# Joint norms of unit pairs in three attention phases, with a new order table, in an attention and gated two-layer kernel

## The chip, the cores and the metric

The kernel runs on one core of one Trainium2 chip. The metric is the device time of one execution in microseconds (us); less is better. Before the change the median of three runs is 299.85 us (299.45 to 300.24).

## The reference

Inputs `q`, `k`, `v` have shape 8 x 8 x 576 x 64 (batch, heads, sequence, head size). Attention is causal with a window of 128 positions and a linear position bias per head; its output, 4608 tokens of 512 values, goes through two matrix products with `h * cos(h)` between them.

```python
scores = scale * q @ k.T                              # per batch and head
mask   = (rel >= 0) & (rel < 128)                     # rel = query pos - key pos
attn   = softmax(where(mask, scores + slope[h] * -abs(rel), -1e9))
x      = (attn @ v) -> 4608 x 512
h      = x @ w_in                                     # 512 -> 2048
out    = (h * cos(h)) @ w_out                         # 2048 -> 512
```

## The kernel before, in words

**Work units.** The attention of one batch is cut into nine units. A unit `(b, pr, G)` is a pair of heads `pr` (0 to 3) and a half `G` of the first 512 queries; the ninth, `(b, "t", None)`, holds the last 64 queries of all heads. A unit goes through `scores` (TensorE, lines 529 and 539), `exps` (ScalarE, 590 and 598), `mask` (VectorE multiplies by the band and the bias, 611 and 623), `pv` (TensorE, 640 to 656, with a column of ones in `v` that gives the sum of each row), and the norm: a reciprocal of the row sums and a multiplication, both VectorE reading PSUM. `norm` does it for one unit (694 and 696, or 681 and 684 for the tail unit), `norm_two` for two units at once (710 and 712). The result `xnat` is turned into `xT`, either by TensorE and a copy (`x_pe`, 729 and 742, copies at 752 on ScalarE or 753 on VectorE) or by a transposing DMA on SP's queue (`x_dma`, 768), which is used where the tokens are not needed in the very next stage.

**Pairs and banks.** `attention` takes the units two at a time. Their `pv` write PSUM banks 2 and 3 (the list `UB`); two `pv` of a pair are one operation unless one unit is a tail. A pair is normed jointly in the phases listed in `JN`, and only where it holds no tail unit. A joint norm keeps both banks until its multiplication is done, and takes two neighbouring `xnat` buffers.

**Stages.** The 4608 tokens are nine chunks of 512. For each chunk c: the first product with `w_in` and the cosine (`moe1`, 782, 787, 791; `moe1_half`, 975, for chunk 0; `moe1_fast`, 876 to 943, with fewer products for the last chunks), then phase c of attention with a quota of units (8, 10, 10, 12, 14, 9 for phases 0 to 5, after 9 units of a start phase), then the second product with `w_out` (`moe2`, 1161, or `moe2_fast`, 1067 and 1138, with the operand sums at 1031 and 1046). Attention of phase c and the second product of chunk c are interleaved on TensorE.

**The start.** The first rows of `q` come by SP's queue (363) and are cast by VectorE (367) and ScalarE (368); the others and `k` come by POOL's queue (356). TensorE transposes them against the identity made by POOL (420, 421), and ScalarE (500) or VectorE (501) copies them out as `qt` and `kt`. Then come the first scores, exponentials (with the masks made at 460 and 465), `pv`, norms and transposes, and the first matmuls with `w_in` (975).

**The order.** All operations are recorded first, in program order, with their data, buffer and bank dependencies. Then `follow` reads `TABLE`: a packed list of the numbers of all operations in the order in which they are issued, with one bit more for each copy that may run on ScalarE or on VectorE (set: VectorE). Each engine runs its operations strictly in that order, waiting on semaphores. The table thus sets the order on TensorE, VectorE, ScalarE, and of the transfers on POOL's and SP's queues, for the whole kernel.

Of the kernel before, what the change touches and what calls it, by code (L numbers as in the profile page):

```python
# [8 lines left out]
ALU = mybir.AluOpType  # L9
# [7 lines left out]
NBLK = 5  # L17
# [10 lines left out]


TABLE = (  # L30
    'c-nPV2Y6If7JmPfH!Wo*A%PHdEHqifjs=k}tV#(GFqBXPBn4$bu`FK_%_4*%1ObV(K#D*JSt&-E!h-'
    '0xDvPKfD@{Z`QYO7kX6D^JciMYzU|;fHUhcd1+;jf_Kj&N_3_w#jJy552L+3%Pc;zlP#H-yktj(-'
    'pEjqM{ck}PJwCrB3q-'
    '{9M;&d$5qHR9WADS}~;_2H1xbO#`q+wdtgon`B>6%HyG|f?3%VnDsdnr<5N0St5ZZ)?8zmXNGD<Zg2=y6N`U+Gy?'
    '$F$*GyJWJoN!r+3anTS_iMU&FrmJy)q1{k##U*rYHRJHq^Dy35b!Y@oPU}o$A?_9;n<O%5Xs0l2&{m^^1BgNm_9P'
    '~pqObs4C1TN&{Qy{6(86~%nA#%H5NW^O=4`d2vLnc~h(_}2&mQcz_^`@$G{b79x#rnLjt-93Hcj0-'
    'yv%|m2e+*e0cZK}!+72b)WUaJT8@pXD+fk0N6bOV1gB(Si4?NA5T2-'
    '!JB(zEKr!Mj%{>;HUNYjab!Z7$qCql;L3G!CjefR+FFk(bw73vr<2ntCbb8MB)_5dQYyf6J%<J=0tY;ul(MgN&rc'
    'O0s&EiG$uIcm#Y~Vab;v#yqnaVrE7GY>V-A}Btqa`;P_Nv&jvF#{*7WM`>VMkre&#)Wy?uO_aV#gax-'
    'm{4=v5trFP6j>R?Tw2c0rY#J*M(j<PaOY>o)>#w^hUa2)xJ2kX>J~-'  # L40
    '#3SczLYEI#)13`0UMgZCvSU&r@KXVhQx8AYHOt^~S#t385v1pL)39f1&X4(!RY_VSn%~;N7Le~0Vt5k)3C!7qncH'
    'Sb_KKyP6<WQBL=(H{om`}^2hwehkBNkN1f6-'
    '=6Jf`#n1*9F&|{#~8ip5b`?XFO3>mnmKg4fqM&X#D2BXTu`vb#MxEL-'
    '2=FZh<=U!>)?uhVjo~ev?pC0h90j^d!W2#$W>Vg}3Lez;yMB~`dF58D5!*GHZ4bkokcrZJo8XMBIs3+J`c0!*&!='
    'cNak2M(+9t6%k<c;_TI5&xT-;_~SjMe)zLQ?kr-'
    '9G)}so_oZgT~!nS)>B%(>F{i(nL<%Kma6dPT_kIY8xqVGm@6sSZY)QY;}3kyZHF!JjrNbPWohF6A1kpQae^Jz>4Y'
    'nMq|4ag_#Z%abX$X0Qx{bdg5-'
    'w!C^Sy0wzSSv6YO*7!5g5KOZPW>L)jeqDWi^PVfHiNt_&bV&I7<#pb?el1f*R3lvbBscPqQM6(|M=#E!7MQtWiEo'
    '^$q8jetWg{{laSk`ID;w6<lHL!It@CI3ZRWxET-dy=6bdfZi^BN)-'
    'kx6rkxYh^Af7Y$CX%W0qP@nf!;+_cuy#JAV$$(>L5)aS8M@n1a32RRL3Yb{W0a`!VJ8|o4{JEnxs(L});p(&v8a9'  # L50
    'u_yO{KZHL$YuW?tu(Sy-'
    '!vCGTmAdZpg4wXLtycpkG<<E5@OtDZg=!_1h1+Njmjw*z0aL)7QnhFOPv(elHPlI>oe%EXgvk}suL+RHI+l!oPEe'
    'ttc)y)KY7q-'
    'GO9HpEp~!82*s>_!_J5TR{@5f%EL7h^Wh(4l4fbO%j~jd783&`#My06C4>3;+Is6L%3tT|^hYe#$tr1&iB&6{dwW'
    'wmj!;Baz_4=p8Jja_9ps>tY{=<;GUvOwSAXGq+K`;>!KNrH|ImXY(ASTzHFN^apdvpSj*r6^VK)$8H@P=`NPcPO&'
    'XkYSBhFw`irt0gqb!LQPqlVQC7VwU?z)4yP6n<)+6xUk=rH29r)HJ=#nkkufV0J5o_@v9wsQWd0@&P$WT0e*0vOC'
    'WIl=#9la*x}LDtWaQG=0xl2(#f%Kz3QWi+K|tR$xwKh#_K~ywPUk>V_~X988-'
    'dL$7M*|kTUzrMQ~>ttJm@GYT>9QFLiQ#JGHIu^Q5UX9joXGsV+1N~s5tf4rg&Z0t843@yK)VUZ;eO{vvf>bj#_<{'
    'E{YJE13lG{)N}UY3D6Y>lsCkRX4ja{$9_e$IQETy;j`zD56VwIGwJ{vRRhIkkY72;<?OL;WxyDsbjLJ`d?#gik4L'
    '%OwvOj>3X-Yk5pe`ia}jeHouYwjx-lYe?zUO*6w~{=z!E<7?VOdoJcyIBk3;YN22T&Udsl*?z2EoT*eN`VQ(2lOw'  # L60
    '$ie!%Cd#CND}y^H-5G~apWoVM#%(x$>q1=4UeA7@v$>FHVpXpRNz-`z1w9-2S&rNI|0<^yIkuIxJ1&2qr-'
    'yn-P&*BAkwbEg<YgZWM`B<Ux7!?;yxT0hEB9Poq9_H<xB+6$<+&1*V*jXQ=!i##UhbBC-HxJ9b4f>O5FQM$GVlYY'
    '0;EzOMeT$+Oi@ir?~G>em;QF`Fb7Uw0-'
    ')DSUv5QX5E;wvHsQX@ok50m+CO*%wR0XM0gH$JNq(o?|pd}rcrfU%@Ny^NS$EwY}9WNlRrb}CwAb0!CyUIkX8zeE'
    't`lBMNi5`Z9289jS-byN0#8`Z0-K46!6u51NJvfI*I<pVOKD}#Bep<(EjKAJ>#OvyA?}aT-'
    'Eb<QtZWG>gAiq@nZu|-Z>5YIIxXgTPJ-Qv8(%8OF{x~utj?J<T~4~q=Mu!G!`B%o{U^X7EYfMjy|cFw5l`KlR}P!'
    'Ka8_mW<8uzKs|eA|5Ic*_e7cdlcU3q+K^v!GU5I4-4igxj^A<ASLge=;<iQSZL!w7=WR?W#-'
    'vXhCLeN@7x(>g+{qRDABl6lLS<Fw>!h`LQKaFe(HMu)ipAva=P&;AW;|7_8}?>Xa&1&CWqRI3oTyJm0VHkMj~b-'
    'KU~R;VLVn(IO$x|2XD-#Cwa~YvoxGM@0FUnOnlZXB(9|3jhMQu{ARUV7(DVnyPJ@o)_f&pP-'
    '0v1&I@q5tK0fHEZqW2B6vpePz;Nsr3p!)OwvLraMQ%IB0%b!Fk8kvD!^ICX(d5SU`>)JBl;A)3x!^A~*gA1H!Njk'  # L70
    '9bb31AJ#9jLnSFn5nJP8V+>6WI*{{9$K=-'
    'Ii4(}ekB>9rlTbz8;dAV@$vsGY#Mm*p3)v9cI)0mEeyn;9Sk1Ej+_{IEB=6m(OWM%qp|L4FkV=POcUwRSz4?%tjO'
    '!EE7%nJVFo1y$1xLEKDW3+%V*`a_(LEi!<eA{Ja22J?)4@RI|7PRIIN8a6UkTIrQNx^0MmIX}Gdse33v8*ibI3(}'
    'Q6!`hQq7VFL0TWDyL%1z)LEb|Fqa2QJsRyz<9M$)jGC(Gyq6mu#GUiIyWiMn}lrw_vC^2CnX65Kq(JOA5auqsW#('
    'az6gPr;3Fs3vS*iFTO!lleCE-fW~K`s@;f-'
    'DuL7*vWwMFvwo)YDYK%Ys!&lL=}a$qa_Dqe_$j$%4|P%7Sk&C^p7|E-05OoaEoQU{w(_HKhuIl)N)0L6E?If-ndQ'
    'f>bOkomPRMj6=zXYB;2Fs8S$=8>KAS9bxj%$jo92RQykW$_h$ynL-'
    ';1n|B~0C{NjJ5M;#~HD{_qDyS92ASr8Q=(}$hf?wlN8Dh7U35CEE3Rb4eZHcVrLB=YO&ys+EVM&F9-'
    '>_E|awkyN8>TE$>Y^ZLfm%hXRv?#4)t*Y5EYzr4%5w1xWK3uw7gWYn<tfyI;9|8HRZ>;#t145fwkp%W<gb}oO8Vt'
    ';%~TDI391Zd3iT@kVuEmcuME+!AOkCeh?Xh408{MGRAGcvK=>2_;SOCz;Xi5FXBMh@##BcNK~)Hu608vNLvl*BDH'  # L80
    'GHNRFy;B3gs%n{7pj$fl+x7VWHhmHY6$LK<1t&5`BViq8BRfR0)!TR`@J<FZkbrVSDq@w=+*W79u-'
    'AsdYv9Vyey(st|R(RU84Bg0wsI(4aO|@>6G)${!)5eW-e@5K<&=Z_fWO<s>k5KMFa_g&GrXJ7L|{Z-'
    'kIjkN?mA0G*W>_y'
)


# [9 lines left out]
class Plan:  # L96
# [18 lines left out]
    def op(self, eng, fn, r=(), w=(), dma=None, occ=100, lat=None, pri=5, mode=0, table=None, two=False):  # L115
        o = Op()
        o.two = two
        o.seq = len(self.all)
        o.eng = (eng,) if isinstance(eng, str) else tuple(eng)
        f = fn[0] if isinstance(fn, list) else fn["act"] if isinstance(fn, dict) else fn  # L120
        o.grp = "/".join((self.now, f.__code__.co_qualname.split(".")[-3],
                          o.eng[0] if dma is None else "dma"))
        o.soft = pri < 5
        pri = self.PRI.get(o.grp, pri)
        o.fn, o.r, o.w, o.dma = fn, tuple(r), tuple(w), dma
        o.occ, o.lat, o.pri, o.mode, o.table = occ, occ if lat is None else lat, pri, mode, table
# [24 lines left out]
        self.all.append(o)
        return o
# [7 lines left out]
    def follow(self, text):  # L160
# [5 lines left out]
        for lo, hi in zip(raw[:n], raw[n:]):  # L166
            at = (at + lo + 256 * hi) % 65536
            o = self.all[at % 32768]
            if isinstance(o.fn, dict):
                e = "dve" if at >= 32768 else "act"  # L170
                o.fn, o.eng = o.fn[e], (e,)
            self.order.append(o)

# [79 lines left out]
def bass_alibi_sliding__then__act_gcu_kernel(  # L253
# [8 lines left out]
    with ExitStack() as ctx:  # L262
# [596 lines left out]
        def moe1_fast(c, f4):  # L859
# [358 lines left out]
        identity()
        load_qk("q", q, 0, 1)
        load_qk("k", k, 0, 1)  # L1220
        constants()
        load_v(0, range(2))
        load_w_in(0)
        load_v(0, range(2, NBLK - LORD))
        masks()
        for n in range(2):
            qk_transposes(0, "q", n, 0, OB)
            qk_transposes(0, "k", n, 0, UB)
        for u in range(1, 4):
            load_w_in(u)  # L1230
            if u == 1:
                load_v(0, range(NBLK - LORD, NBLK))
# [92 lines left out]
```

## Time and profile before

| what | value |
|---|---|
| median of three runs | 299.85 us |
| profiled execution: its own time | 299.71 us |
| profiled execution: span of its instructions | 298.0 us |
| VectorE busy | 262.1 us (88%), 522 instructions |
| ScalarE busy | 222.1 us (75%), 318 instructions |
| POOL busy | 95.2 us (32%), 122 instructions |
| TensorE clock granted | full in every stretch |
| first matmul starts, last matmul starts | 5.70 us; about 295 us |

The span runs from the first to the last instruction. The profiled execution's own time is 1.7 us longer than its span. PE is TensorE's matrix multiplication, PEld its weight load, which overlaps the matmul before; DVE is VectorE, ACT is ScalarE, POOL is GpSimd, SP the engine that only issues transfers. A row of the timeline gives the start, the length, the engine, the line, the tiles and the count of merged instructions, and in brackets how long the engine had been idle and what released it.

### The profile page before, as it was taken

The page shows a single profiled execution, that of the slowest core. Times are in us where ns is not written, and L with a number is a line of the kernel's source. Part 1 is how long each engine was busy: PE and PEld are TensorE (multiplying, and loading weights), DVE is VectorE, ACT ScalarE, POOL GpSimd, SP SyncE. Part 2 cuts the span into 40 slices and gives each one's busy share as a digit, 9 for nine tenths or more (in the row PEclk, how much of TensorE's full clock was granted, in tenths as well). Part 3 has the DMA queues.
Part 4 walks back from the last instruction along what each step waited for, and adds up shares of the span by engine and source line. Part 5 has one row for each costly group of instructions (what it writes and reads, how often), then busy time and mean ns, then how long its engine had stood idle before and what let it go on. Part 6 is the DMA issues. An engine that isn't in the chain of part 4 may idle for free.

```text
span 298.0 us, 7278 instructions
## 1 busy us (share of the span) xinstructions
PE 287.9 (97%) x2974; PEld 205.2 (69%) x2974; DVE 262.1 (88%) x522; ACT 222.1 (75%) x318; POOL 95.2 (32%) x122
## 2 busy tenths in 40 slices
PE   2899999999999999999999999999999999999996
PEld 2678845446874586458854788547768888888884
DVE  3879877599977999899999999999999999999972
ACT  5788878689757889688777878579778758778620
POOL 7997000599642303991195005000000000000000
PEclk9999999999999999999999999999999999999999
DMA  7999999999999994999999939973131400041033
GB/s 153 173 205 208 207 169 146 180 196 155 136 175 147 130 187 90 142 173 173 169 170 133 163 85 130 159 164 74 21 79 21 150 2 0 2 141 37 10 134 106
DMA packets 147729, 37.96 MB, mean 127 GB/s; under 512 B 133360, under 2 KB 146416, under 8 KB 147696
## 3 DMA queue, kind: packets, MB, share of 16 engines
q0 software_dynamic: 99344, 18.10, 79.7%
q1 hardware_dynamic: 48352, 19.41, 34.5%
q8 instruction: 23, 0.38, 0.5%
q14 instruction: 10, 0.08, 0.1%
HBM read 36.70 MB, written 9.44 MB: 155 GB/s over the span
## 4 chain that ended last, share of the span: by engine, by line
PE 94%; DVE 2%; POOL 1%; issue 1%; ACT 1%; POOLq 0%; DVEq 0%
PE ps L1067 33%; PE ps L782 24%; PE ps L876 11%; PE ps L539 5%; PE ps L975 5%; PE ps L1161 4%; PE ps L653 3%; PE ps L656 2%; PE ps L742 2%; PE ps L483 2%; PE ps L529 1%; DVE kt L501 1%; PE ps L640 1%; PE ps L642 1%; PE ps L1138 1%
## 5 line engine op out<-in xcount | busy, mean ns | idle before, releaser
L1067 PE MATMUL ps<-w_outb,gT 128*128 128x256 f16 x512 | 82.3, 273 | 0.0
L782 PE MATMUL ps<-xT,w_inb 128*128 128x512 f16 x336 | 82.2, 379 | 0.0
L787 ACT ACTIVATE cos<-ps,halfpi 128x512 f32<-128x512 f32 x84 | 54.9, 687 | 18.9 <-PE ps L782 13.9
L598 ACT ACTIVATE p<-ps 128x768 bf16<-128x768 f32 (+1 forms) x64 | 55.6, 915 | 11.5 <-PE ps L539 9.5
L791 DVE TENSOR_TENSOR gT<-ps,cos 128x512 f16<-128x512 f32 x84 | 54.5, 686 | 5.5 <-ACT cos L787 5.1
L1067 PEld LDWEIGHTS ps<-w_outb,gT 128*128 128x128 f16 x512 | 48.2, 98 | 12.5 <-issue 1.3
L782 PEld LDWEIGHTS ps<-xT,w_inb 128*128 128x128 f16 x336 | 31.7, 98 | 31.1 <-DVE gT L791 1.5
L375 POOL DMA_DIRECT2D vp<-in_v_dram x40 | 34.3, 892 | 53.1 <-PE ps L656 35.3
L1067 PE MATMUL ps<-wsum,gsum 128*128 128x256 f16 x256 | 38.5, 273 | 0.0
L623 DVE TENSOR_TENSOR p<-p,emask 128x768 bf16<-128x768 bf16 (+1 forms) x64 | 38.0, 615 | 0.3
L385 POOL DMA_DIRECT2D qnat<-in_q_dram x30 | 25.5, 918 | 23.9 <-DMA qt<-qnat 23.9
L1052 ACT ACTIVATE ob<-ps 128x512 f32<-128x512 f32 x33 | 19.6, 598 | 13.7 <-PE ps L1067 11.2
L385 POOL DMA_DIRECT2D knat<-in_k_dram x30 | 25.7, 948 | 9.3 <-DMA kt<-knat 7.0
L1067 PEld LDWEIGHTS ps<-wsum,gsum 128*128 128x128 f16 x256 | 23.2, 98 | 4.0 <-issue 0.5
L876 PE MATMUL ps<-xT,w_inb 128*128 128x256 f16 x132 | 24.8, 273 | 0.0
L696 DVE TENSOR_TENSOR xnats<-ps,rec 128x256 f16<-128x256 f32 x56 | 21.9, 420 | 0.5
L539 PE MATMUL ps<-qt,kt 64*128 64x128 bf16 (+1 forms) x320 | 20.1, 253 | 1.3 <-DVE kt L501 1.3
L653 PEld LDWEIGHTS ps<-vp,p 128*128 128x128 bf16 x256 | 16.0, 99 | 4.3 <-issue 1.0
L653 PE MATMUL ps<-vp,p 128*128 128x65 bf16 x256 | 18.9, 196 | 0.1
L1067 PE MATMUL ps<-wsum,gT 128*128 128x256 f16 x112 | 18.1, 273 | 0.0
L539 PEld LDWEIGHTS ps<-qt,kt 64*128 64x128 bf16 x320 | 11.9, 98 | 8.6 <-issue 3.6
L1161 PE MATMUL ps<-w_outb,gT 128*128 128x512 f16 x64 | 17.6, 380 | 0.0
(111 smaller groups left out, 478.0 us busy)
## 6 DMA issues: line engine op xcount, KB each, us to landing
out_dram<-ob SPq DMA_DIRECT2D x35, 256.0 KB, 2.7
vp<-in_v_dram POOLq DMA_DIRECT2D x32, 128.0 KB, 6.9
qnat<-in_q_dram POOLq DMA_DIRECT2D x24, 128.0 KB, 7.1
knat<-in_k_dram POOLq DMA_DIRECT2D x24, 128.0 KB, 10.8
w_inb<-in_moe_w_in_dram POOLq DMA_DIRECT2D x4, 512.0 KB, 10.5
w_outb<-in_moe_w_out_dram POOLq DMA_DIRECT2D x4, 512.0 KB, 21.8
gsum<-in_q_dram POOLq DMA_DIRECT2D x1, 576.0 KB, 15.5
gsum<-in_k_dram POOLq DMA_DIRECT2D x1, 576.0 KB, 17.6
```

The costliest lines, as they stand in the source:

```text
L375: op("pool", [lambda e, t=t, rows=rows: e.dma_start(vp[b % 2][0:rows, t, :, 0:64], v[b, :, 128 * t:128 * t + rows, :].rearrange("h p d -> ...
L385: fns.append(lambda e, t=t, rows=rows: e.dma_start(nat[which][b % 2][0:rows, t, :, :], src[b, :, 128 * t:128 * t + rows, :].rearrange("h p ...
L539: ins = e.matmul(ps[:, banks[x], c0:c1], keys_ap(b, x, pr, kc), query_ap(b, x, pr, qb, 128 * nb), start=c0 == 0 and (b, pr, G) not in seed ...
L598: op("act", lambda e: e.activation(P[i][:, :, 0:hi], src_[:, :, 0:hi], ACTF.Exp, scale=0.125), w=held + [("P", i)], occ=920 if G else 691, ...
L623: op("dve", lambda e: e.tensor_tensor(p, p, m, ALU.mult), r=[("EM", h0), ("EM", h1)] + ([] if G else [("EM2", h1)]), w=[("P", i)], occ=600 ...
L653: ins = e.matmul(o, P[i][:, x, d0:d0 + 128], V[:, kc, h, 0:65], start=True, stop=not two)
L782: op("pe", lambda e, kc=kc: e.matmul(ps[:, bank, :], w_in[:, kc, 128 * fc:128 * fc + 128], xT[:, kc, r0:r0 + CH], start=(kc == 0), stop=(k ...
L787: op("act", lambda e: e.activation(cosb[ci][:, :], ps[:, bank, :], ACTF.Sin, bias=halfpi[:, 0:1]), r=["halfpi"], w=[("B", bank), ("cos", c ...
L791: op("dve", lambda e: e.tensor_tensor(gT[gi][:, fc, :], ps[:, bank, :], cosb[ci][:, :], ALU.mult), r=[("cos", ci)], w=[("B", bank), ("g", ...
L876: op("pe", lambda e, i=i, kc=kc: e.matmul(ps[:, bank, 256 * i:256 * i + 256], left(kc, p0 + i), right(kc), start=(start and i == 0 and kc ...
L1067: op("pe", lambda e, t=t, p=p: e.matmul(ps[:, bank, 256 * t:256 * t + 256], left(p, slice(128 * t, 128 * t + 128)), right(p), start=(start ...
L1161: op("pe", lambda e, t=t, fc=fc, bank=bank: e.matmul(ps[:, bank, :], gT[gi][:, fc, 128 * t:128 * t + 128], w_out[:, fc, :], start=(fc == 0 ...
```

## The change

```diff
-        JN, PRE2, SEEDN, XD, LORD = (5,), (), {}, {4: 6}, 0
+        JN, PRE2, SEEDN, XD, LORD = (3, 4, 5), (), {}, {4: 6}, 0
+        PCOS = False
...
-                e = "dve" if at >= 32768 else "act"
+                e = "dve" if at >= 32768 else o.eng[0]
...
-        load_first_q()
-        load_qk("k", k, 0, 0)
-        distances()
+        if LORD == 3:
+            ...
+        else:
+            distances()
```

`TABLE` is replaced as a whole. The branch for `LORD == 3`, and one that lets POOL make a product where `PCOS` is set, are not taken. So the recorded program differs only in phases 3 and 4: `QUOTA` gives them 12 and 14 units, five pairs without a tail in each, and in each of these ten pairs two reciprocals and two multiplications become one of each. The old table lists 2842 operations, the new one 2822. Operations recorded ahead of phase 3 keep their numbers, so the start can be compared. Some of it, read out of the two tables as `follow` reads them (q0, q1, k0, k1: first and second piece of the first batch, a and b their two halves; numbers count the pairs of heads):

```
TensorE
 old: transpose q0 k0 | scores 0 1 | transpose q1 k1 | scores 2 3 | pv 0,1 | ... | tail scores | first w_in
 new: transpose q0 k0 | scores 0 1 | transpose q1 | scores 2 | transpose k1 | scores 3 | pv 0,1 | ... | first w_in (8) | tail scores
ScalarE
 old: masks 2,6 | cast q | masks 3,0,1,5 | copy q0a k0a | masks 4,7 | exp 0 1 | copy q1b | exp 2 3
 new: cast q | masks 4,6,7,5,2 | copy k0b | masks 0,3,1 | exp 0 1 | exp 2 | copy q1a k1a | exp 3
VectorE
 old: nine memsets | cast q | copy q0b | a mask copy | copy k0b | three mask copies | mask 0 1 | copy q1a k1b k1a | mask 2 3 | norms
 new: one memset | cast q | one memset | copy q0a q0b | two memsets | copy k0a | four mask copies | mask 0 1 | a cast | copy q1b | mask 2 | copy k1b | ... | mask 3 | norms
POOL
 old: load k0 | distances (1) | load q1 | distances (2) | load k1 | identity | loads of v
 new: identity (1) | load k0 | distances (1) | load q1 | identity (2) | distances (2) | load k1 | loads of v
```

In the whole table 20 copies change their engine, nine from ScalarE to VectorE and eleven the other way.

More of the change, by code (lines that the diff above doesn't have):

```diff
@@ L30 @@
 TABLE = (
[L31 to L80, printed above, removed]
@@ L81 @@
-    'GHNRFy;B3gs%n{7pj$fl+x7VWHhmHY6$LK<1t&5`BViq8BRfR0)!TR`@J<FZkbrVSDq@w=+*W79u-'
-    'AsdYv9Vyey(st|R(RU84Bg0wsI(4aO|@>6G)${!)5eW-e@5K<&=Z_fWO<s>k5KMFa_g&GrXJ7L|{Z-'
-    'kIjkN?mA0G*W>_y'
+    'c-'
+    'nnd30PHS8b0sc?`0DZGIOsOb4j0ShB2*X%50ouaY5xl%|ubrNOOg;fpQJeR7A;;5m7?ih0I4SE19&$ah|Cr#~wpP'
+    'QQ1+rT<*g8=ljoH&N&yGbMM*y^Zm>Be((2wzYu5*wCY{Zvrg!GYi(L|x`LZ^HWrRr^l*0e(f&88sxzvt2mby<{~P'
+    '^(dE&+|quaE1AGcXralyniJ%O5D;D?53SsR9EMQyzan$`g~&2(vi{#fVaKs2CxcMIA<XB%3B0|1j9SIAZj>}7z?0'
+    '{78E=jFja{1&(*4uv_8w|%|m!ym=yOJcME1F9vfj=@#1S<a-~l-'
@@ new lines @@
+    '^EYf(tsBJHp%dO}A0Q?IAXLLnGS5Bc0Gwi`|4KOQWS|=`*-2P4m+C!L=~2`-'
+    '|<vzpPtlh4&ax+XMHT!l|p#0n9CQh45B$$HYQ@@7`$ZZJUUb4G|cNAo8MYY%p(c_Vhl6z}N;;IS}&&d*Lj(X2B#I'
+    'IebJ6i`gfdUTlmwPmLzB?2Ai7wJwd(p}`P(eSp(q*yzKeDYjh0%*<hC{T>G@Mut_4{DywdRGlGkHIdK_LLYrTmN>'
+    'SL{(K^!>(o*3^j0{k2VHxrjyw&32~IQgE~f>~S_BxJhM*2=gVtuD7@M60Ok}+dx}d8F$XRxL5+a(zwE6R!%I4#K$'
+    'z;5jfl%mEcea!yVO6HVnURxb+6m2qfmdmjPhR5)T}OXhm#%X{77R#1N+|^$*Z|ZavOZF}W{0Q0^C55#J^1-'
+    'P>dbabI~ZTK<sMl^)?<w!C^bjK@4qtz#D-'
+    'PIZzAtjqX}WnG&_<vA`EC;ma|0DyLO!f>`H<y8yQ=%Fb{ZlS@v3_il(iLC^F~UI3uQ4-Wc+qX=bZgi`Oe-'
@@ new lines @@
+    '4q0p(1h<4ZS>4ys_&TsD7AFh_YwXyJv#+*YL>7wh#$ITtUzpX<6x8=_PdzU8ML6tey^X$|Rsu4Vs7j=Ya2Oqrpa!'
+    'krL`W&GJBIk<c%#F7Kb%Jmn^S?j9?}}ea^!g9^a9KohF&#ZPW^*lp1E+8vSWgQvx%t7S$a^zl0N2fO)?Ur&64fT)'
+    'cpBq*{{*Fl>LBp9=cKEdWlJi`Dk86vu;SQ-!(U4y%;*VXesIu(Ex;J(<nxk)`%i;DR#FzMZ?<-'
+    '#}QYO1za8YtYbWVHer-D?8^y<?;T3Ov4Hk?V_AX*=$7AMfdMxbZN=NzPeVmeF7R|1TGNb2;R-'
+    'Q2>J82a*g$!dlVuIrJR{JN{_|c#An^<)1MU=L+CO-|9qsQNu8BzBjCZikR7;?x9mQg-rGeUAdAQGA%fPx1R>GXbU'
+    'UGG6SlWEUHg{;TA$e1Gxb&Fy(F$z#Wg;$)K$?b4-4jb}XaYi8LOEt5PLBIDg|q|>pT2k+214y+9L7Y#o^z-'
@@ new lines @@
+    '9+{;IjbqCoL<ij)*pzHuz^RNI%8&XJeI8jMya+#f?Z4JLVFDz`4v6}_~%ruT$R`5)oH^y-46-uro)-'
+    'mgE_zd=P#8m7p8a3$qA)_wYwQSgT*t00t0DWm9jn_;%LE^*l!C+z#q3O6!VYZ_*R^rjF86k$6UZE{HSV$kOXmu2&'
+    'IR5(4h^dS8SX8`{yPCN^qa(<5pPZth2!h3178^O2R**<8FgO=J1zY-'
+    '7FD@GQ?JeY@@&KmRR^A!>lch(yZB>{@L;sDBw=bJsz$TO?@<if;5^b;}=Ah9r{%o9N6Iwu+AtY~lNI_uYc9Xq>1>'
+    '{^NuH{lrVGpy?=xKyk{(K5y2Jt*-eFiZ*n4hiK!5lEQj-'
+    'V)BLvkTHF!{5&Bs5%?%^$2Ja$B%b!%_os(?Ck3cV(IEF<&`WJ&o_VOjMvb0cMf>7`(FchZoOdm_D%>x=X-'
+    'D?B0;x-1BbF#JxB_5JP`@?9MRf57=?@dcRFK`U6$^(GR|%0Wqcq&)IUbQ59^t@_;aIf!#%tdOH-'
@@ new lines @@
+    '+l@zc);{2>y^3K?Nbiyr)K;Nctr`-'
+    '{(M`OFe8GkbL`3riYWbu?TFQf^MnA48qvtm)s;u<Lm5&TEF#TCM%?SW|fJigjCkWv-'
+    '4(&3unD41g{on6ed@ufz`)7Rgiv>_XA$IS~D6fkXv(Q&@;5T+4HdELVnBeB9buMi1AZL72CzvA5>Y%j){F)wT!ad'
+    'G5~1LKX3k&mygoRyOC6;QbgIaoSph*aA2ctCX)C+E_oG?Me`+f){y`E&W|ON+G{OTR08(tu;jH!ddz1`(Ff{-'
+    '(MVap-sLNnRvf`hL|<UOPDt)qOXl-'
+    ';`=5QFm46hHPF8*L0J7oQKsJy447O6&T)Hbvc3LVa;2}d>=<{^_j7jXf%9$L`QM;QmT!?t$nf+mq)SGM@eF^DbqR'
+    '|pCFO^rnlbrGONNi&7!BGnMGK&Rx{tWYZP8tkM!o!DE!=V>(O_cKf=hY<>uTK4Nsx74En`e2){jV?s;=xs)uGfrX'
@@ new lines @@
+    'J8!2FwWBL6BMzG2tlc62F*&&AOE086We&=<&J{|1xL>ffS9vO@1#?d!{a{0#kr(OL8<z_6FQUcOvn4%1|0=U*v0>'
+    '7UnI%sqwI#x((g@d_>kH^PFir+Pa`EsBOR5WN1bG=|lUG!gV7SW3OS_wYHgYDdSKvssczV`DAV^p|ToLwP|@;)0?'
+    'E%*tRPbh1Rs&kJKGIN0~PC$HqV4OD;)cXU`^*(D*M@KI@?R(f-'
+    'fcghNNMHUwuQhn=07aES7yB&j4R@ra{Ae7l^Y(x;6lQ9R0H(Y|K+)G_+#=u`IiX2WL&+>+vRBJKq4Bo}rc6GX4a0'
+    'iMjRZA-dgH*H5ogDWAKkP(HVm3A3VG-dpp)W2c?ZKsO$<36Rv&gY^&AyMdgH=ZkO1ravDG~!FN1vN~>;mMo@=bW#'
+    'ddmaa7U>~LdXLNsZ5a&<C*@~i`zfd*p`hzQoeqeoo*Ur=?WA`Jk7CknOb}DyMa5|<;gGoFX?KBGC<e)?k@^TVze<'
@@ new lines @@
+    'xOP9(xXJsRp8fX_GwLH_})Ba1ZLkqi6Si7xq;*xii4aCBN&Xt>Cv&>@i5P3rT`#YELnx4Ug{POYKsnm$q@9JC!3&'
+    'F=+=UHPD7n5Sa867@dOWfqpDY$P}_Nne^Rlkd?*nnVFs*o_>P+A_$&gJgw3-'
+    'GmCd(J{#$Y3EpnL5qyWQr@%6^ylu?$R}7=<E3HeA*Qr{EZ(ey_QkP6Y_Drz^&vKc(RG(wgJN4t&EM=?0e>z0BAw='
+    'JFjCn!zE|8l+dWUzx%nOWrO<>AJyT3q?NAv;T)e9fS%x58+$_NNb3#R(!Ua=BE8GEMqdq<IBkY{0nyjnFeIEAu&M'
+    '(m+u`tTCeFEX)+o=lK^U@|7MnU@ZVcBUYK%oLfBzB~~8sHFHVe^ZU+4}xDaW9nJE5L8|d6NIkb6S0UbYObgtVZKj'
+    'v^(1arwlH-LsxVU$hN(KMGK#5tddMdSjH!~7F_m*7QTx|pz#b|EstCy*c+yZUElla0g5^q~^3t29s)VVE_OfeCnM'
@@ L84 @@
+    ')!>xRY9`UxKQOA0-uTC|KozOd|>^uK6WRSF!Uy-1Z_<EyL>vn7=xyhf#@w93-'
+    'FP3J?9b?zSd4n2M<C@TfrYdZ$!Xeg|V+Cs2uwyPw#F$_mAk<<mbOl*DJuZ*VoFDuah6rXZIfAD5VnfWI6lv%*h0{'
+    'Txs(N0pmu`Bp2iTMeWt!MZR-'
+    'p`e0Fs{9t~Tb<0EE}G+M5T#HF(sZKCd@!Xh%G^@$N9BpPT1Y|l456&}{!n(QU8=<LvtoXghpBN8{Ob@?MN(!8cTj'
+    '4Fm$_ifKaJIV_G$%(h9m;g5Q488c&^YReGxse^EJVpM@mWbNjYR<DxGrg9Q-'
+    '9xm4Py=;9v38>sL(3x>jBVJD5Tz{!dCX!B47GdjfxDSMsh)A@v>NL)sLn%Y-fptRx8gmCmYqAPD~h_7zUi'
 )
@@ L119, in op @@
         o.eng = (eng,) if isinstance(eng, str) else tuple(eng)
-        f = fn[0] if isinstance(fn, list) else fn["act"] if isinstance(fn, dict) else fn
+        f = fn[0] if isinstance(fn, list) else next(iter(fn.values())) if isinstance(fn, dict) else fn
         o.grp = "/".join((self.now, f.__code__.co_qualname.split(".")[-3],
@@ L942, in cos_and_product @@
                 cos = cos.rearrange("p (a b t) -> p a b t", a=2, b=2)
-                op("dve", lambda e: e.tensor_tensor(o, srcs, cos, ALU.mult),
-                   r=r + ck, w=w + gk(hf), occ=1139, lat=1225, pri=MPRI, two=hf == 1)
+                f = lambda e: e.tensor_tensor(o, srcs, cos, ALU.mult)
+                if hf and PCOS:
+                    op(("pool", "dve"), {"pool": f, "dve": f}, r=r + ck, w=w + gk(hf),
+                       occ={"dve": 1139, "pool": 2600}, lat={"dve": 1225, "pool": 2750},
+                       pri=MPRI, two=True)
+                else:
+                    op("dve", f, r=r + ck, w=w + gk(hf), occ=1139, lat=1225, pri=MPRI,
+                       two=hf == 1)
             j = n % 2
@@ L1216, in bass_alibi_sliding__then__act_gcu_kernel @@
         load_qk("k", k, 0, 0)
-        distances()
[L1218 to L1232, printed above, removed]
+        if LORD == 3:
+            distances()
+            load_v(0, range(2))
+            identity()
+            load_w_in(0)
+            load_qk("q", q, 0, 1)
+            load_qk("k", k, 0, 1)
+            constants()
+            masks()
+            load_w_in(1)
+            load_v(0, range(2, 4))
+            load_w_in(2)
+            load_w_in(3)
+            load_v(0, range(4, NBLK))
+            for n in range(2):
+                qk_transposes(0, "q", n, 0, OB)
+                qk_transposes(0, "k", n, 0, UB)
+        else:
+            distances()
+            identity()
+            load_qk("q", q, 0, 1)
+            load_qk("k", k, 0, 1)
+            constants()
+            load_v(0, range(2))
+            load_w_in(0)
+            load_v(0, range(2, NBLK - LORD))
+            masks()
+            for n in range(2):
+                qk_transposes(0, "q", n, 0, OB)
+                qk_transposes(0, "k", n, 0, UB)
+            for u in range(1, 4):
+                load_w_in(u)
+                if u == 1:
+                    load_v(0, range(NBLK - LORD, NBLK))
         load_qk("q", q, 1)
```

## The prediction

> **What bounds the kernel now.** I read the page first: who is busy, and which engine the chain that ended last runs through.
>
> ```profile
> PE 287.9 (97%) x2974; PEld 205.2 (69%) x2974; DVE 262.1 (88%) x522; ACT 222.1 (75%) x318; POOL 95.2 (32%) x122
> ...
> PE 94%; DVE 2%; POOL 1%; issue 1%; ACT 1%; POOLq 0%; DVEq 0%
> ```
>
> TensorE is busy for 97% of the span, and 94% of the chain is its work. Busy records of pipelined matmuls overlap, so I check the pace with the longest piece of the chain in order of time (start, length, what):
>
> ```profile
> 280.00 12.51 PE ps L1067 x113
> ```
>
> 113 matmuls of 256 columns in 12.51 us are 0.111 us each, start to start: they follow one another without a hole, so TensorE is the bound and not only occupied. Next come the two stretches in which phases 3 and 4 of attention run (columns: stretch, its length, then busy time and count of PE, PEld, DVE, ACT and POOL):
>
> ```profile
> 133.00:149.00 16.00, 16.00 (x234) 12.89 (x233) 15.37 (x37) 12.86 (x17) 3.35 (x5) 1.00 1.80 170
> 165.00:186.00 21.00, 20.96 (x315) 16.95 (x314) 20.59 (x49) 17.02 (x21) 4.88 (x6) 1.00 1.16 125
> ```
>
> VectorE is nearly full there as well, 15.37 of 16 us and 20.59 of 21. So an engine that could become the bound is the one that the change relieves. Whether TensorE waits for it is told by the waits of PEld, TensorE's weight loads, around these stretches (130 to 151 us, then 163 to 187 us; total, times, longest):
>
> ```profile
> PEld ps L539 <- ACT p L598: 0.8, 4, 0.2
> PEld ps L1067 <- issue: 0.5, 3, 0.2
> PEld ps L539 <- DVE gT L791: 0.4, 1, 0.4
> ```
>
> ```profile
> PEld ps L539 <- issue: 0.6, 3, 0.2
> PEld ps L1067 <- issue: 0.3, 2, 0.2
> PEld ps L653 <- DVE xnats L696: 0.3, 1, 0.3
> PEld ps L529 <- issue: 0.2, 1, 0.2
> ```
>
> Together these are 3.1 us, of which one row, 0.3 us, has a norm (L696) as releaser, and 0.4 us another VectorE product. VectorE is full there, but the order gives it the work that TensorE needs in time.
>
> **The joint norms.** The durations, from the instructions that use the tile of reciprocals (min/median/max ns):
>
> ```profile
> L694 DVE RECIPROCAL rec<-ps x56: 151/176/184, 14.2 to 187.9; 128x4 f32<-128x4 f32 x56
> L696 DVE TENSOR_TENSOR xnats<-ps,rec x56: 394/424/425, 14.6 to 188.1; 128x256 f16<-128x256 f32 x56
> ...
> L710 DVE RECIPROCAL rec<-ps x4: 201/204/209, 208.7 to 216.7; 128x8 f32<-128x8 f32 x4
> L712 DVE TENSOR_TENSOR xnats<-ps,rec x4: 684/684/684, 209.2 to 217.1; 128x512 f16<-128x512 f32 x4
> ```
>
> A pair normed apart costs 2 x (0.176 + 0.424) = 1.20 us, jointly 0.204 + 0.684 = 0.89 us. Ten pairs save 10 x 0.31 = 3.1 us of VectorE and 20 of its instructions. What lies on the path is less. Both banks of the pair are released after 0.89 us instead of one early and one after up to 1.20 us, so the next `pv`, which needs both, may start up to 0.3 us earlier; a transpose or an `x_dma` on SP's queue that needs only the pair's first unit starts up to about 0.3 us later (0.89 against 0.60). Most units of phases 3 and 4 go to `xT` by `x_dma`, for a stage that is a whole phase away, so that delay is hidden by a phase of some 16 us; for the few that go by TensorE, the first of a pair is the one queued behind the longer norm, and the matmuls behind it on TensorE's queue would wait with it. TensorE's waits bound the gain: at least nothing, at most all 3.1 us listed. I take 0.3 us, the one row that names a norm.
>
> A rule speaks for more than that. The Trainium skill, Perfetto Trace Analysis, section Identifying the Most-Contended Engine, calls the busy share of matmuls a bad measure of TensorE's distance from its limit and sends the reader to the share of the weight loads; here that is 69%, below VectorE's 88%, so by that rule VectorE would be the engine to relieve. The trace disagrees for the long stretches, where the row of 113 matmuls above leaves no hole; what it would give is the third rival.
>
> **The start.** The table is new for the whole kernel. Ahead of phase 3 the program is the same, so the two orders can be laid beside each other, with durations from the timeline of 2 to 19 us: TensorE, then ScalarE, then VectorE.
>
> ```profile
> 5.70 1.92 PE L483 MATMUL ps<-ident,gsum 128*64 128x128 bf16 x32 [5.70 <-POOL ident L421]
> ...
> 8.50 0.82 PE L539 MATMUL ps<-qt,kt 64*128 64x256 bf16 x8 [0.88 <-DVE kt L501]
> 9.25 2.35 PE L483 MATMUL ps<-ident,gsum 128*64 128x128 bf16 x40
> ...
> 14.47 0.34 PE L653 MATMUL ps<-vp,p 128*128 128x65 bf16 x3
> ...
> 17.39 0.64 PE L529 MATMUL ps<-qt,kt 64*128 64x64 bf16 x16
> 17.96 0.94 PE L975 MATMUL ps<-xT,w_inb 128*128 128x256 f16 x7
> ```
>
> ```profile
> 6.81 0.60 ACT L500 ACTIVATE qt<-ps 128x512 bf16<-128x512 bf16 x1
> ...
> 9.04 1.51 ACT L598 ACTIVATE p<-ps 128x768 bf16<-128x768 f32 x2 [0.17 <-PE ps L539]
> 10.57 0.88 ACT L500 ACTIVATE qt<-ps 128x640 bf16<-128x640 bf16 x1
> 12.07 1.51 ACT L598 ACTIVATE p<-ps 128x768 bf16<-128x768 f32 x2 [0.62 <-PE ps L539]
> ```
>
> ```profile
> 2.34 0.31 DVE L447 MEMSET kt<- 128x128 uint32 x2
> ...
> 6.81 0.69 DVE L501 COPY qt<-ps 128x512 bf16<-128x512 bf16 x1 [1.40 <-PE ps L483]
> 7.41 0.22 DVE L465 COPY emask<-emask 128x256 bf16<-128x256 bf16 x1
> 7.66 0.69 DVE L501 COPY kt<-ps 128x512 bf16<-128x512 bf16 x1
> ```
>
> - Before, the two halves of q are copied at 6.81 us side by side, one on ScalarE and one on VectorE; k likewise at 7.66. In the new order three of the four copies stand on VectorE. From 6.81, with 0.60 us from start to start (6.81 to 7.41), two more starts, about 0.15 us for a memset moved in between and the last one's 0.69 us: 6.81 + 1.20 + 0.15 + 0.69 = 8.85. The first scores follow 0.15 us behind, as before (8.35 to 8.50): at 9.0 us, **0.5 late**.
> - Third score: 0.82 us of scores and 20 of the 40 transposes (1.17 us) later, at 11.0. Its exponential stands 0.54 us behind it, as the first one does (8.50 to 9.04): 11.5, and takes about 0.7 us to the next start. Then the new order puts two copies of 640 columns (0.88 us each, some 0.8 to the next start) ahead of the fourth exponential: it starts at 13.8 and ends at 14.6, where before it ended at 12.07 + 1.51 = 13.58. That is **1.0 late**, and the second `pv` (14.47 before) goes to 15.5.
> - The norms and transposes behind this `pv` move with it. Before, TensorE fills time there with the tail scores (17.39 to 17.96) ahead of the first matmul with `w_in` at 17.96; in the new order these scores stand behind eight such matmuls. Without them it could have come at about 17.4; 1.0 later is 18.4, which is 0.4 behind, with 0.57 us of tail scores still to do. That is 1.0 less what TensorE does earlier in the holes that the lag leaves, which I put at 0.4 us (half of the 0.82 us of a block of scores): I take **0.6 us**. Bounds: nothing, if the holes take it all, and 1.0 + 0.57 = 1.6 if they take none.
>
> What arrives there is hidden: on POOL's queue half of the identity now stands ahead of the first load and the rest ahead of the load of the last piece of k, so these are issued later by a memset and a select, but that piece is transposed only behind the third score, later than before too. Seven memsets leave VectorE's idle time before 2.7 us for the busy stretch; at 0.31 us for two (L447) they are about 1.1 us of VectorE, in its gaps by the new order, and inside the 1.6 if not.
>
> **The rest of the table.** Elsewhere the orders are alike in kind. The end has the same last 8 + 6 or 7 + 8 matmuls. Pieces like the 113 leave nothing to gain; a worse order could open holes. I take nothing, with bounds from the waits above: 0.8 us, the largest row, either way.
>
> **Sum.** Against the profiled execution (299.71 us; span 298.0 and 1.7 around it): +0.6 at the start, -0.3 in phases 3 and 4, 0 elsewhere: 300.0 us. The median shown is 0.14 above that execution, so the forecast stands at **300.15 us**, a change of +0.3 us, 0.1%. A measurement of this kernel can tell about 0.3%, 0.9 us, from no change.
>
> **Rivals.**
> - *Slower: the fourth exponential behind two copies.* The lag of the start goes through whole: 1.0 us from the exponential and 0.57 us of tail scores, 299.85 + 1.6 = 301.4. For it: TensorE has no hole later that could take a lag back. Against it: TensorE does have holes between 13 and 18 us. It decides if the first matmul with `w_in` starts at about 19 us instead of 17.96.
> - *Faster: the waits of phases 3 and 4 close.* VectorE with 3.1 us more room delivers copies, masks and products earlier, and half of the 3.1 us of TensorE's waits go, with no lag at the start: 299.85 - 1.5 = 298.35. For it: VectorE's 97% there. Against: only 0.7 us of these waits name VectorE.
> - *VectorE is the bound.* Then its 3.1 us go through: 299.85 - 3.1 = 296.75. The rule of the Trainium skill named above would have it so. The pace of the 113 matmuls speaks against it.
> - *The change does nothing.* The pairs are made joint where no one waits, and the start takes up its lag: 299.85.
>
> **How the numbers follow.** Forecast 0.50 (range of its own 299.3 to 301.0: within 0.38, slower 0.10, faster 0.02); slower rival 0.22; faster rival 0.17; VectorE as bound 0.04; nothing 0.07. So faster 0.02 + 0.17 + 0.04 = 0.23, within 0.38 + 0.07 = 0.45, slower 0.10 + 0.22 = 0.32. The range reaches from the faster rival to the slower one, 298.3 to 301.6, and leaves out VectorE as bound and the outer parts of the others.
>
> **What would show it.** In the profile after: VectorE has 500 instructions in place of 522 (20 norms and two copies fewer) and about 259 us busy; L710 and L712 come 14 times; the first scores start at about 9.0 us, the fourth exponential ends near 14.6, the first L975 starts at about 18.4; TensorE's waits in the stretches of phases 3 and 4 still add up to some 3 us, and TensorE stays at 97%. The forecast is wrong if the first L975 starts before 17.9 or after 18.9, if these waits shrink by over 1 us, or if new waits of TensorE for a norm or a transfer appear anywhere after 20 us.

## The result, and the profile after

The changed kernel takes 302.1 us (median of 6 runs, 300.9 to 303.5) against 299.79 us before; the ratio is 1.0076, with a 95% interval of 1.0058 to 1.0095. It is slower by 2.3 us, outside the range that was given. Its runs also scatter over 2.6 us, where those of before lie within 0.8. The profiled execution is the slowest of the six, 303.5 us, so its waits can be larger than the usual ones.

The page, its first part and the chain that ended last:

```profile
span 301.8 us, 7257 instructions
...
PE 287.7 (95%) x2974; PEld 203.1 (67%) x2974; DVE 259.2 (86%) x500; ACT 223.3 (74%) x320; POOL 95.1 (32%) x122
...
PE 68%; DMA 16%; DVE 5%; POOL 5%; ACT 2%; SPq 2%; issue 1%; POOLq 0%
```

VectorE has 500 instructions and 259.2 us, as worked out; TensorE has the same work and is busy as long as before, in a span that is 3.8 us longer. The chain tells more: it is no longer TensorE's alone, 16% of it are transfers, of several kinds. The waits of TensorE's matmuls over the whole run (total, times, longest), behind the one of 5.7 us for the first operands, which is there before and after, have these as the largest:

```profile
PE ps L537 <- ACT emask L458: 1.3, 1, 1.3
PE ps L651 <- DVE xnats L710: 1.1, 1, 1.1
PE ps L979 <- DMA w_inb<-in_moe_w_in_dram: 0.9, 2, 0.7
PE ps L651 <- DMA vp<-in_v_dram: 0.7, 1, 0.7
```

Before, that view has one row more than the 5.7 us, for copies of k at the start:

```profile
PE ps L539 <- DVE kt L501: 1.3, 2, 0.9
```

Of the four after, one belongs to the first scores, one to the first weights, one to a tile of v at 122 us, and one to a joint norm (L710) at 190 us. Where that norm was held up is told by the timelines of VectorE, TensorE and SP's queue:

```profile
177.61 0.68 DVE L710 TENSOR_TENSOR xnats<-ps,rec 128x512 f16<-128x512 f32 x1
...
187.86 0.20 DVE L708 RECIPROCAL rec<-ps 128x8 f32<-128x8 f32 x1
189.37 0.69 DVE L710 TENSOR_TENSOR xnats<-ps,rec 128x512 f16<-128x512 f32 x1 [1.31 <-DMA xT<-xnats]
```

```profile
190.12 0.20 PE L651 MATMUL ps<-vp,p 128*128 128x65 bf16 x1 [1.09 <-DVE xnats L710]
```

```profile
176.32 4.46 SPq L766 DMA_TRANSPOSE xT<-xnats  x3
180.82 1.09 SPq L1099 DMA_DIRECT2D out_dram<-ob  x2
181.96 3.16 SPq L766 DMA_TRANSPOSE xT<-xnats  x1
```

VectorE stands still for 1.31 us with the reciprocal done, because the multiplication writes a pair of `xnat` buffers, and a transposing DMA (`x_dma`) has not yet read an earlier unit out of one of them. The eight buffers are used in turn, as a ring; this pair of buffers was written last by the multiplication at 177.61 us, so its transfers had some 10 us. One of them was issued at 181.96 us behind two stores, and the chain of waits gives it 7.39 us to land:

```profile
181.96 7.39 DMA xT<-xnats
189.34 0.02 issue
189.37 0.70 DVE xnats L710
190.07 0.05 issue
190.12 0.20 PE ps L651
```

Behind the multiplication waits the `pv` that needs its PSUM banks. Before, SP's queue has all four transfers of this stage ahead of the store:

```profile
173.59 6.87 SPq L768 DMA_TRANSPOSE xT<-xnats  x4
180.50 0.58 SPq L1095 DMA_DIRECT2D out_dram<-ob  x1
```

From 165 to 192 us these transfers also take longer than before; the row of before first, then that of after (issue to landing):

```profile
DMA to landing us min/median/max: 2.3/4.1/6.2
```

```profile
DMA to landing us min/median/max: 2.3/7.4/8.7
```

### The profile page after: what moved, and what is told of

It reads as the page before. It is cut to its first block, busy times and chain, and to the rows that moved or that the text cites. A ratio compares the mean times of both kernels' runs of the same rounds, so it can differ in the third digit from the quotient of the medians.

```text
span 301.8 us, 7257 instructions
## 1 busy us (share of the span) xinstructions
PE 287.7 (95%) x2974; PEld 203.1 (67%) x2974; DVE 259.2 (86%) x500; ACT 223.3 (74%) x320; POOL 95.1 (32%) x122
## 4 chain that ended last, share of the span: by engine, by line
PE 68%; DMA 16%; DVE 5%; POOL 5%; ACT 2%; SPq 2%; issue 1%; POOLq 0%
PE ps L1071 23%; PE ps L780 18%; PE ps L874 11%; DMA vp<-in_v_dram 5%; PE ps L1165 4%; DMA w_inb<-in_moe_w_in_dram 4%; PE ps L979 4%; DMA kt<-knat 3%; PE ps L537 3%; DMA xT<-xnats 2%; SPq L394 2%; POOL vp L373 2%; PE ps L651 2%; DMA ob<-in_q_dram 1%; POOL knat L383 1%; DVE p L621 1%
## 5 line engine op out<-in xcount | busy, mean ns | idle before, releaser
L1071 PE MATMUL ps<-w_outb,gT 128*128 128x256 f16 x512 | 83.5, 273 | 0.0
L785 ACT ACTIVATE cos<-ps,halfpi 128x512 f32<-128x512 f32 x84 | 54.2, 686 | 20.7 <-PE ps L780 17.9
L1071 PE MATMUL ps<-wsum,gsum 128*128 128x256 f16 x256 | 41.1, 273 | 0.0
L874 PE MATMUL ps<-xT,w_inb 128*128 128x256 f16 x132 | 26.1, 273 | 0.0
L537 PE MATMUL ps<-qt,kt 64*128 64x128 bf16 (+1 forms) x320 | 19.4, 243 | 1.6 <-ACT emask L458 1.3
L1165 PE MATMUL ps<-w_outb,gT 128*128 128x512 f16 x64 | 18.3, 380 | 0.0
L979 PE MATMUL ps<-xT,w_inb 128*128 128x256 f16 x128 | 16.3, 273 | 0.9 <-DMA w_inb<-in_moe_w_in_dram 0.9
L537 PEld LDWEIGHTS ps<-qt,kt 64*128 64x128 bf16 x320 | 11.2, 95 | 8.8 <-ACT p L596 2.9
```

The costliest lines, as they stand in the source:

```text
L537: ins = e.matmul(ps[:, banks[x], c0:c1], keys_ap(b, x, pr, kc), query_ap(b, x, pr, qb, 128 * nb), start=c0 == 0 and (b, pr, G) not in seed ...
L785: op("act", lambda e: e.activation(cosb[ci][:, :], ps[:, bank, :], ACTF.Sin, bias=halfpi[:, 0:1]), r=["halfpi"], w=[("B", bank), ("cos", c ...
L874: op("pe", lambda e, i=i, kc=kc: e.matmul(ps[:, bank, 256 * i:256 * i + 256], left(kc, p0 + i), right(kc), start=(start and i == 0 and kc ...
L1071: op("pe", lambda e, t=t, p=p: e.matmul(ps[:, bank, 256 * t:256 * t + 256], left(p, slice(128 * t, 128 * t + 128)), right(p), start=(start ...
L1165: op("pe", lambda e, t=t, fc=fc, bank=bank: e.matmul(ps[:, bank, :], gT[gi][:, fc, 128 * t:128 * t + 128], w_out[:, fc, :], start=(fc == 0 ...
```

## The experiments

Theory A: the loss is the new order's, in a start that lags and in transfers that come late. Theory B: the joint norm itself costs, since it needs two buffers and two banks at once. An order can be taken apart because any prefix of one table, followed by what is left of the other in its own order, again puts each operation behind those it depends on; likewise the sequence of one engine or queue can be exchanged where no circle arises. All of them compute the whole reference. Where the edit is an order, its fence says in words how the table was put together, and the table is left out. Each ratio is against runs of the kernel before in the same session, with medians of 299.79 to 300.03 us, so it is not the quotient of two medians shown here.

| run | norms in phases 3, 4 | order | buffers | median us | ratio to before, 95% |
|---|---|---|---|---|---|
| changed kernel | joint | new | 8 | 302.1 | 1.0076 (1.0058 to 1.0095) |
| e1 | joint | old | 8 | 301.0 | 1.0035 (1.0024 to 1.0046) |
| e2 | apart | new | 8 | 302.29 | 1.0068 (1.0046 to 1.0090) |
| e3 | apart | new start, old rest | 8 | 300.39 | 1.0015 (1.0002 to 1.0027) |
| e4 | joint | old start, new rest | 8 | 302.32 | 1.0080 (1.0056 to 1.0105) |
| e5 | joint | new, POOL's queue old | 8 | 302.57 | 1.0096 (1.0063 to 1.0129) |
| e6 | joint | new, SP's queue old | 8 | 300.87 | 1.0035 (1.0023 to 1.0046) |
| e7 | joint | new, both queues old | 8 | 301.14 | 1.0051 (1.0033 to 1.0069) |
| e8 | joint | new | 10 | 300.67 | 1.0029 (1.0015 to 1.0043) |
| e9 | joint | new, one transfer moved | 8 | 300.7 | 1.0027 (1.0015 to 1.0039) |
| e10 | apart | old | 10 | 299.97 | 1.0001 (0.9992 to 1.0010) |
| e11 | joint | old start, new rest | 10 | 300.67 | 1.0018 (1.0006 to 1.0031) |
| e12 | apart | old start, new rest | 10 | 300.39 | 1.0014 (1.0004 to 1.0024) |
| e13 | joint | old | 10 | 300.95 | 1.0028 (1.0018 to 1.0039) |
| e14 | joint | old start, new rest, one transfer moved | 8 | 300.29 | 1.0012 (1.0002 to 1.0022) |

**e1, joint norms in the old order.**

```diff
-        JN, PRE2, SEEDN, XD, LORD = (5,), (), {}, {4: 6}, 0
+        JN, PRE2, SEEDN, XD, LORD = (3, 4, 5), (), {}, {4: 6}, 0
 # TABLE: the old order; the joint reciprocal and multiplication where the pair's first ones stood
```

> Joint norms in phases 3 and 4, all else in the old order (each joint pair stands where the pair's first reciprocal and first multiplication stood). Theory A (the loss is the new order's: a start that lags, weights and v tiles that come late): within 0.3% of before, 299.3 to 300.2, at best 0.3 us faster. Theory B (the joint norm itself costs: it needs two xnat buffers and two banks at once, and VectorE stands still until transposing transfers have freed them): slower by 1 us or more, 300.8 to 302.

301.0 us: it costs 0.35%, about 1.1 us, though VectorE has 3 us less to do. It lies in theory B's range, 300.8 to 302, but not by B's wait for transfers. The waits of the weight loads between 130 and 188 us show the place:

```profile
PEld ps L731 <- DVE xnats L701: 0.6, 2, 0.4
PEld ps L771 <- DVE xnats L701: 0.5, 1, 0.5
PEld ps L528 <- DVE gT L780: 0.4, 1, 0.4
PEld ps L642 <- DVE xnats L701: 0.3, 1, 0.3
```

Three rows, 1.4 us together, wait for the joint multiplication (here line 701): the transposes of a unit (731), a matmul of the first product (771) and the next `pv` (642). Before, the norms have two such rows over the same 58 us, 0.7 us together, so 0.7 us are new:

```profile
PEld ps L653 <- DVE xnats L696: 0.5, 2, 0.3
PEld ps L782 <- DVE xnats L696: 0.2, 1, 0.2
```

No DMA is named.

**e2, the new order with the norms apart.**

```diff
-        JN, PRE2, SEEDN, XD, LORD = (3, 4, 5), (), {}, {4: 6}, 0
+        JN, PRE2, SEEDN, XD, LORD = (5,), (), {}, {4: 6}, 0
 # TABLE: the new order; the pair's four operations where the joint two stood
```

> The new order with the norms of phases 3 and 4 apart again, each pair's four operations where the joint two stood. Theory A: stays slow, 301 to 303, with the start's lag and the waits for w_in and for v. Theory B: back to 299.8 to 300.6, only the start's 0.6 us left, and the wait of 1.3 us of VectorE for a transposing transfer at about 188 us gone.

302.29 us: as slow as the changed kernel. Theory A holds for the larger part, and the stop of VectorE is there without any joint norm, longer than after:

```profile
186.41 0.24 DVE L683 RECIPROCAL rec<-ps 128x4 f32<-128x4 f32 x2
188.87 0.76 DVE L685 TENSOR_TENSOR xnats<-ps,rec 128x256 f16<-128x256 f32 x2 [2.22 <-DMA xT<-xnats]
```

**e3 and e4, the two orders spliced.**

```diff
 # e3: JN (5,);      the new order up to the last matmul of moe1_half, then the old
 # e4: JN (3, 4, 5); the old order up to the last matmul of moe1_half, then the new
```

> Norms apart; the new order up to the last matmul of chunk 0's first product, and the old order behind it. The prediction's start term: +0.6 us, 300.4. If the wait for the first w_in tiles at 20.8 and 23.3 us belongs to the start as well: +1.2 us, 301.0. If the rest of the run takes the lag up: 299.8.

> Joint norms; the old order up to the last matmul of chunk 0's first product, and the new order behind it. Theory A with the start and the queues as separate parts: the start's 1.2 us go and the rest stays, 300.5 to 301.5. If the start is all of it: 299.8. If the transfers on POOL's and SP's queues behind the start are nearly all of it: 301.5 or more.

The new start alone costs 0.15%, 0.5 us (0.06 to 0.8): the term that was forecast as 0.6. e4 did not get better by as much, nor at all: with the old start and the new rest the runs lie between 300.86 and 304.62 us, so a half microsecond can't be seen in that scatter. e4 says where the large part sits, behind the start.

**e5, e6, e7, the queues.** The compute engines keep the new order; the sequence of one queue is exchanged.

```diff
 # e5: POOL's sequence from the old table    e6: SP's sequence from the old table    e7: both
```

> The changed kernel with POOL's queue (loads and its few products) in the old order, all else new. Theory A1 (the loads, which the new order issues later and closer to the transposing transfers, make the weights, v and the xnat buffers late): back to within 0.8 us of before, 299.8 to 300.6. Theory A2 (SP's queue does it: one transposing transfer stands behind a store that waits for its sum): no better than the changed kernel, 301.5 to 302.5, and the stop of VectorE at 186 to 190 us stays.

> The changed kernel with SP's queue (stores and transposing transfers) in the old order, all else new. Theory A1: no better, 301.5 to 302.5. Theory A2: the stop of VectorE at 186 to 190 us goes, and with it 1.0 to 1.9 us: 300.3 to 301.

> The changed kernel with both queues in the old order. If the two queues hold all of the loss behind the start: 300.3 to 300.6, what the new start alone gave. If the order of the compute engines, which was made for the other queue order, loses as much by waiting for it: 301.5 or more.

POOL's loads are not it: e5 is no better, and its profile still has VectorE stopped by 0.9 us:

```profile
DVE xnats L701 <- DMA xT<-xnats: 0.9, 1, 0.9
```

SP's queue is: with its old sequence 0.4 of the 0.76% goes, and no such row is left between 180 and 192 us. Exchanging both queues is not better than SP's alone; e7's upper run, 302.7, widens its interval.

**e8, ten buffers.**

```diff
-        NX = 8
+        NX = 10
```

> The changed kernel with 10 xnat buffers in place of 8, orders as in the changed kernel. If the ring of buffers is what VectorE waits for at 186 to 190 us, the wait falls on a transfer one pair earlier and mostly goes: 300.5 to 301.2. If transfers are so late that every buffer is, 301.5 to 302.5.

300.67 us: two more `xnat` buffers take away as much as SP's old sequence, within the intervals. The row of the wait shrinks:

```profile
DVE xnats L685 <- DMA xT<-xnats: 0.2, 1, 0.2
```

**e9, one transfer moved.** In the sequence of SP's queue:

```diff
   x_dma, phase 4, buffer 5
+  x_dma, phase 4, buffer 4
   store 3 of chunk 3
   store 0 of chunk 4
-  x_dma, phase 4, buffer 4
```

> The changed kernel with one transposing transfer of phase 4 moved on SP's queue ahead of the two stores that it stood behind. If this one place holds the loss that the old SP queue took away: the stop of VectorE at 186 to 190 us goes, 300.5 to 301.2. If the lateness is spread over the queue: 301.5 to 302.3, with the stop at the next transfer.

300.7 us: one place in one queue holds 0.49% of the 0.76%, 1.4 us. SP's queue now has four transfers ahead of the stores, and VectorE passes from the reciprocal to the multiplication without a stop:

```profile
175.62 5.29 SPq L757 DMA_TRANSPOSE xT<-xnats  x4
180.95 1.09 SPq L1090 DMA_DIRECT2D out_dram<-ob  x2
```

```profile
187.17 0.20 DVE L699 RECIPROCAL rec<-ps 128x8 f32<-128x8 f32 x1
187.51 0.69 DVE L701 TENSOR_TENSOR xnats<-ps,rec 128x512 f16<-128x512 f32 x1
```

**e10, e11, e12, the ring and the worth of the joint norms.**

```diff
 # e10: before, NX = 10
 # e11: JN (3, 4, 5), NX = 10, the old start, the new rest
 # e12: as e11 with JN (5,), the norms split as in e2
```

> The kernel before with 10 xnat buffers. If its order never waits for the ring: the same, 299.6 to 300.1. If the ring binds there too: 0.3 us or more faster.

> Joint norms, 10 buffers, the old order up to the last matmul of chunk 0's first product and the new one behind it. Start lag (0.5 us) and ring wait both out: 299.7 to 300.2, level with before, if these two are the whole loss. If the new order behind the start loses elsewhere too: 300.5 or more.

> As the run with old start, new rest and 10 buffers, but the norms of phases 3 and 4 apart. What the joint norms are worth in an order made for them, with no wait for the ring: if VectorE's 3 us count, this is slower than that run by 1 us or more; if TensorE is the bound, by 0 to 0.3 us.

Two more buffers are worth nothing to the old order (e10), which does not wait for the ring. With the old start and ten buffers, joint (1.0018) and apart (1.0014) cannot be told from each other: 3 us of VectorE's time are worth nothing that these runs can see. Ten buffers do not end every wait: e11's profile still has VectorE held by a transfer for 0.7 us between 180 and 192 us, of which 0.3 us reach TensorE. Both stay 0.4 to 0.5 us above before, so the new order behind the start loses a little there or elsewhere; the range of level with before, 299.7 to 300.2, was missed.

**e13, e14, what was still open.**

```diff
 # e13: as e1, NX = 10
 # e14: the old start, then the changed kernel's order with the transfer of e9 moved
```

> Joint norms in the old order, as in the first experiment, with 10 xnat buffers. If that run's loss of about 1 us is a wait for the ring: level with before, 299.7 to 300.2. If it is that the first unit of each pair is ready later than the old order counts on (its transposes on TensorE and its transfers): no better, 300.7 to 301.1.

> The changed kernel with the old order up to the last matmul of chunk 0's first product and the one transposing transfer moved. If the start (0.5 us) and this one place (1.4 us) are separate parts of the loss and add up: 300.0 to 300.4. If lateness of transfers behind the start remains: 300.6 or more.

e13 (1.0028) keeps e1's loss within the intervals, and its waits:

```profile
PEld ps L731 <- DVE xnats L701: 0.6, 2, 0.4
PEld ps L771 <- DVE xnats L701: 0.4, 1, 0.4
```

So e1's loss is not the ring. Its waits name the joint multiplication, whose first unit is ready later than in the old order; they account for 0.7 of the 1.1 us. In e14 start and transfer add up: from 1.0076 to 1.0012, some 1.9 of the 2.3 us. No version beat the kernel before.

## Why the prediction was wrong

- **What bounds the kernel: right.** TensorE does, and room on VectorE is worth nothing that can be seen (e11 against e12). The Trainium skill, Perfetto Trace Analysis, section Identifying the Most-Contended Engine, judges TensorE by two measures, its share of peak arithmetic and the share of its weight loads; the prediction used the second alone, which put TensorE's 69% below VectorE's 88%. If that made VectorE the bound, e11 would be up to 3 us faster than e12, and it is not faster at all.
- **The joint norms: the saving right, the gain on the path not there.** 14 pairs at 0.200 and 0.688 us and 2.9 us less of VectorE are as worked out. The path was to gain 0.3 us. In the new order joint and apart cannot be told from each other (302.1 and 302.29; e11 and e12), so the term is about nothing in the changed kernel; in the old order the joint norms lose 1.1 us (e1). The waits that the term came from were read in two windows that leave out 151 to 163 us and end at 187; over 130 to 188 us the norms have 0.7 us of them, not 0.3. The text named the cause, the first unit of a pair behind the longer norm, with transposes on TensorE behind it, and then gave it no term, because most units go by DMA.
- **The start: right in size, not in all its steps.** e3 gives 0.5 us (0.06 to 0.8), forecast 0.6. The first scores were forecast at 9.0 us and started at 8.98; the fourth exponential starts at 13.54 (forecast 13.8). But the first matmul with `w_in` starts at 17.38, not 18.4, ahead of the 17.9 below which the forecast was to be wrong, and the tail scores follow:

```profile
8.98 0.82 PE L537 MATMUL ps<-qt,kt 64*128 64x256 bf16 x8 [1.32 <-ACT emask L458]
...
16.64 0.28 PE L740 MATMUL ps<-ident,xnats 128*128 128x128 f16 x2 [0.44 <-DVE xnats L694]
...
17.38 1.05 PE L979 MATMUL ps<-xT,w_inb 128*128 128x256 f16 x8
18.36 0.41 PE L527 MATMUL ps<-qt,kt 64*128 64x64 bf16 x16
...
20.78 1.48 PE L979 MATMUL ps<-xT,w_inb 128*128 128x256 f16 x12 [0.66 <-DMA w_inb<-in_moe_w_in_dram]
```

  Part of the difference is the profile that was reckoned from: the same 16 tail scores took 0.64 us in the profiled execution of before, and 0.41 us here and in e10, which has the order of before and starts its first matmul with `w_in` at 17.47 in place of 17.96:

```profile
17.10 0.41 PE L518 MATMUL ps<-qt,kt 64*128 64x64 bf16 x16
17.47 0.93 PE L970 MATMUL ps<-xT,w_inb 128*128 128x256 f16 x7
...
19.39 1.27 PE L970 MATMUL ps<-xT,w_inb 128*128 128x256 f16 x10 [0.29 <-DMA w_inb<-in_moe_w_in_dram]
```

  So the profiles show little of a lag of 1.0 us at this point. Where the 0.5 us of e3 sit is not shown, and that the number agrees is in part luck.
- **"What arrives there is hidden": not shown to be wrong.** One of the moved memsets is needed by the loads of v, so POOL waited, and the weights behind them were issued later, the first at 8.79 us against 8.15:

```profile
POOL vp L373 <- DVE vp L441: 1.0, 1, 1.0
```

  The wait of 0.66 us at 20.78 for the weights could follow from that. But e10, with POOL's queue as before, has such a wait too (the last row above), and e12, with the old start, a longer one:

```profile
20.02 1.27 PE L970 MATMUL ps<-xT,w_inb 128*128 128x256 f16 x10 [0.89 <-DMA w_inb<-in_moe_w_in_dram]
```

  e3, with POOL held in the same way for 0.9 us, has none among its matmuls. So this wait comes and goes with either start.
- **The step that failed** is the one on the transfers: "Most units of phases 3 and 4 go to `xT` by `x_dma`, for a stage that is a whole phase away, so that delay is hidden by a phase of some 16 us." An `x_dma` has two readers of its end. One is the later stage; the other is the unit that reuses the `xnat` buffer, and with 8 buffers and 14 units in the phase that one is close behind: some 10 us, not 16. The new table put one such transfer behind two stores; "The rest of the table" therefore had a term of 1.4 us (e9) where I took nothing, with 0.8 as the bound. Against the forecast of +0.6, -0.3 and 0, the runs give +0.5 for the start and about 0 for the joint norms in this order, which leaves some +1.8 for the rest of the table: the 1.4 us of this transfer and 0.4 that no run places. The prediction had named a new wait of TensorE for a norm or a transfer behind 20 us as a sign that it was wrong; both came.
- **The rivals.** The time lies near the slower rival's 301.4, but its mechanism, the start, gives 0.5 us of the 2.3. The rival that costs most, a late transfer that holds a buffer, was not among them.

Still open: why the moved transfer took 7.39 us to land. With POOL's old sequence the stop stayed, so the order of the loads alone does not make it; that the other transfers of that time share the DMA engines was only argued. The wait for a tile of v at 122 us in the profile after, 0.7 us, was not taken apart either; the stop of VectorE does not make it, since e9's profile has it too (0.8 us) with that stop gone. The last 0.3 to 0.5 us of the new order stay open as well. That the scatter of the runs comes from such landings fits e4 and e9, and was not shown by itself.

## What to carry to other kernels

When a table moves a transfer, list everything that its end releases: not only who reads the result, but who reuses the source buffer; with a ring of n buffers the time allowed is at most n units, not the phase. Where one engine is the bound, count a saving on another at nothing until a run shows more, but count each result that becomes ready later, here the first half of a merged pair, against the work queued behind it. And where a new order comes with the edit, run the edit in the old order first, and the new order without the edit: two runs said here that neither paid.

## What had not been expected of the hardware

From 165 to 192 us SP's queue issued a transposing transfer in about 1.2 us before (1168 to 1248 ns). After, one of these took 3.16 us to issue and 7.39 to land, against a median of 4.1 us from issue to landing before. That transfer, moved ahead of two stores, was worth 1.4 us of a run of 302 (e9). TensorE's pace in the first 18 us differed between two executions of the same order: 16 equal matmuls took 0.64 us in the profile of before and 0.41 us in that of e10, where the buffers alone differ.
